# One opening transfer, half-width first products, a root on GpSimd and a new order in a fused attention and MLP kernel

## The chip, the cores and the metric

The kernel runs on one core of a Trainium2 chip. The metric is the device time of one execution in microseconds (us). The kernel before takes 588.61 us, the median of 3 runs (588.04 to 588.75). A core has five engines with an instruction queue each: TensorE (PE; its weight loads are listed as PEld), VectorE (DVE), ScalarE (ACT), GpSimd (POOL) and SyncE (SP), which issues the DMAs. An engine works through its queue in order, so an instruction that waits holds up all that stand behind it.

## The reference

Two batches of 768 tokens, 8 heads of 64. Attention is local (96 keys back) plus the first 8 keys, with a distance bias, then two feed-forward blocks of width 2048, the first with a scale and an offset:

```
n_global, n_local = (8, 96)
scores = scale * q @ k^T;  keep = is_global | is_local
bias = -slopes[:, None, None] * dist[None]
a = exp(where(keep, scores + bias, -1e9) - max) ;  a = a / (sum(a) + 1e-09)
x = (a @ v) laid out as [1536 tokens, 512]
r = max(x @ w_in, 0);   x = (s * (r * r) + b) @ w_out        # moe,  s and b are one number each
r = max(x @ w_in2, 0);  out = (r * r) @ w_out2               # moe2
```

## The kernel before, in words

**Tiles.** The 1536 tokens are 12 tiles of 128 rows; tiles 0 and 1 are the first of each batch and see 128 keys, the others 192. For each tile `qk` makes scores on PE, `ttr` adds the bias and takes the extreme on DVE, `exp` runs on ACT, `rsum` and `norm` divide, `tr` transposes on PE, `tput` copies the result out of PSUM (the tile `at`), `pv` multiplies by v, and `xhi`/`xlo` split the result in a high and a low part (`xh`, `xl`). Weights come as 64-bit numbers in 64 transfers of 512 KB (`st`), are decoded in four steps (`wdec`, steps 0 to 3), and split by `whi`/`wlo`. A product of split numbers is three matmuls: high by high, high by low, low by high.

**Stages.** The first four blocks of 128 columns of the first MLP (`h`, `relu`, `square`, `ghi`, `glo`, `y`, 256 tokens at a time) run woven into the attention, up to about 100 us; then the other blocks of both MLPs run by a seven-product scheme (`product`, 384 tokens) and its output matmuls (`y2`). The last output rows are finished one by one (`yrow`, six rows m of 128 tokens), added to what was kept (`flush2`) and stored.

**Order.** `order` lists every piece of work with its engines, an assumed cost, what it depends on and a due time; `Plan.run` places the pieces on the engines and so writes each engine's queue. `SHIFT` moves due times of single pieces, `PIN` binds a piece to an engine. Where PE has nothing to do before the first `h`, the planner writes small idle matmuls (`warm(0)`, 256 columns of zeros) into its queue. None of this is decided on the chip: there the queues run as they are written.

**The opening.** SP issues the transfer of n (L1408), then that of s and b (L1419), both spread over 128 partitions, then q and k of tile 0 (L410), the first weight block (L39), v and tile 1. DVE converts n (L1414 to L1416), starts the square root of s (`root`, L818 to L829), builds the bias planes (`consts`, L353 to L371), and then begins with `ttr` (L444).

Of the kernel before, what the change touches and what calls it, by code (L numbers as in the profile page):

```python
# [17 lines left out]
DM = H * D  # L18
DFF = 2048
P = 128  # L20
# [8 lines left out]
WARM, FILL = 8, 0.2  # L29
TB, SB = 768, 384  # L30
# [30 lines left out]
def decoded(a):  # L61
# [9 lines left out]
SHIFT = {('at', 2, 2): 28.4, ('at', 2, 3): 26.5, ('at', 3, 0): 33, ('at', 3, 1): 42, ('at', 4, 1): -16.3, ('at', 5,  # L71
    0): 6.4, ('at', 8, 0): 57.6, ('cadd', 14, 1, 1, 0): 225.2, ('cadd', 18, 0, 1, 0): 201, ('cadd', 20, 0, 1, 0):
    135.6, ('cadd', 26, 0, 0, 1): 288.3, ('cadd', 6, 0, 0, 1): 148.7, ('cadd', 8, 0, 0, 1): 237.2, ('check', 0):
# [21 lines left out]
    -34.3, ('ndh', 0, 3): -76.6, ('ndh', 0, 7): -33.3, ('ndh', 1, 0): 29.9, ('ndh', 1, 3): -2.7, ('ndh', 1, 5):  # L95
    -101.2, ('norm', 11, 3): -1.5, ('norm', 2, 1): -255.6, ('norm', 3, 1): -138.7, ('norm', 3, 2): 0.3, ('norm', 4,
# [1386 lines left out]
```

## Time and profile before

| what | us |
|---|---|
| median of 3 runs | 588.61 (588.04 to 588.75) |
| the profiled execution | 588.15 |
| its span, first to last event | 586.3 |
| PE busy (98% of the span) | 575.1 |
| DVE busy (84%) | 492.6 |
| ACT busy (61%) | 359.8 |
| POOL busy (16%) | 94.9 |

Busy shares are means over very different stretches, so they are read stage by stage: what stands still at the opening, which engines are full while attention and MLP are woven together, and what is left behind the last matmul. Matmuls overlap in their pipeline, so the time that one takes of PE is the distance between the starts of neighbours and not its own duration. The page's chain of waits is empty for this run; the bound is read from the stretches and from the timelines of the queues. The span does not hold 1.85 us of the execution's time.

### The profile page before, as it was taken

How to read it: one execution, taken by the hardware profiler on the slowest of the kernel's cores; microseconds unless marked ns; L12 is line 12 of the kernel's file. 1: busy time of each engine (PE TensorE's matmuls, PEld its weight loads, DVE VectorE, ACT ScalarE, POOL GpSimd, SP SyncE). 2: the span in 40 equal slices, each digit the busy share in tenths (PEclk: the TensorE clock that was granted, in tenths of full speed). 3: DMA queues.
4: the chain of work that ended last, by engine and by line, in shares of the span. 5: the costliest groups of instructions: out<-in, count | busy, mean ns of one | idle time of the engine just before them, and what ended most of it. 6: DMA issues, size and time to landing. Idle time of an engine off the chain costs nothing.

```text
span 586.3 us, 11064 instructions
## 1 busy us (share of the span) xinstructions
PE 575.1 (98%) x4125; PEld 520.3 (89%) x4125; DVE 492.6 (84%) x1139; ACT 359.8 (61%) x820; POOL 94.9 (16%) x176
## 2 busy tenths in 40 slices
PE   6999999999999999999999999999999999999997
PEld 4688988999989999999999989989899889989895
DVE  6999997699999899999989999899886987874443
ACT  4999987685766666556566666657454535444330
POOL 3653434101100000110000012120112011200000
PEclk9999999999999999999999999999999999999999
DMA  6876621032120332314021301323222131100023
GB/s 262 314 240 243 221 93 37 3 109 69 40 74 0 109 108 72 108 34 147 11 99 36 108 0 37 108 79 101 72 73 66 44 108 59 49 0 2 15 94 110
DMA packets 14888, 52.12 MB, mean 89 GB/s; under 512 B 1904, under 2 KB 2160, under 8 KB 14832
## 3 DMA queue, kind: packets, MB, share of 16 engines
q1 hardware_dynamic: 14832, 51.39, 25.8%
q8 instruction: 33, 0.54, 0.4%
q14 instruction: 23, 0.19, 0.1%
HBM read 48.24 MB, written 3.15 MB: 88 GB/s over the span
## 4 chain that ended last, share of the span: by engine, by line


## 5 line engine op out<-in xcount | busy, mean ns | idle before, releaser
L645 PE MATMUL h<-xh,u 128*128 128x384 f32 x448 | 130.5, 337 | 0.0
L748 PE MATMUL yy<-u,gh 128*128 128x512 f32 x360 | 111.9, 392 | 0.0
L645 PE MATMUL h<-th,u 128*128 128x384 f32 x336 | 99.6, 337 | 0.1
L742 PE MATMUL yy<-gh,u 128*128 128x512 f32 (+1 forms) x384 | 98.4, 337 | 0.0
L645 PEld LDWEIGHTS h<-xh,u 128*128 128x128 f32 x448 | 82.3, 188 | 1.1
L748 PEld LDWEIGHTS yy<-u,gh 128*128 128x128 f32 x360 | 67.0, 188 | 11.8
L645 PE MATMUL h<-xl,u 128*128 128x384 f32 x224 | 75.4, 336 | 0.0
L742 PEld LDWEIGHTS yy<-gh,u 128*128 128x128 f32 x384 | 66.7, 189 | 7.7
L748 PE MATMUL yy<-u,gl 128*128 128x512 f32 x180 | 70.3, 391 | 0.0
L742 PE MATMUL yy<-gl,u 128*128 128x512 f32 (+1 forms) x192 | 64.8, 338 | 0.3 <-DVE gl L719 0.3
L645 PEld LDWEIGHTS h<-th,u 128*128 128x128 f32 x336 | 62.0, 188 | 2.4 <-DVE u L666 0.8
L274 ACT ACTIVATE u<-st 128x512 fp32r<-128x512 f32 (+1 forms) x58 | 36.5, 634 | 39.1 <-DVE st L57 25.5
L645 PE MATMUL h<-tl,u 128*128 128x384 f32 x168 | 56.5, 336 | 0.0
L278 POOL TENSOR_SCALAR u<-st 128x512 fp32r<-128x512 f32 (+1 forms) x34 | 25.1, 739 | 171.9 <-PE h L645 61.8
L54 DVE SCALAR_TENSOR_TENSOR st<-st 128x512 int32<-128x512 int32 x64 | 45.1, 705 | 3.7 <-ACT gh L714 0.5
L274 ACT ACTIVATE st<-st 128x512 f32<-128x512 f32 x64 | 42.3, 677 | 7.7 <-DMA st<-in_moe_w_in_dram 3.8
L57 DVE SCALAR_TENSOR_TENSOR st<-st 128x512 int32<-128x512 int32 x64 | 44.1, 690 | 1.0
L645 PEld LDWEIGHTS h<-xl,u 128*128 128x128 f32 x224 | 42.1, 188 | 0.8
L452 ACT ACTIVATE sn<-sn,nm 128x192 f32<-128x192 f32 (+1 forms) x96 | 41.8, 444 | 0.2 <-DVE nm L444 0.2
L748 PEld LDWEIGHTS yy<-u,gl 128*128 128x128 f32 x180 | 33.8, 188 | 7.4
L666 DVE TENSOR_TENSOR u<-h,m 128x384 f32<-128x384 f32 x56 | 30.9, 552 | 11.2 <-PE h L645 10.0
L679 DVE TENSOR_TENSOR u<-h,u 128x384 f32<-128x384 f32 x56 | 30.9, 552 | 11.1 <-PE h L645 10.6
(163 smaller groups left out, 1206.9 us busy)
## 6 DMA issues: line engine op xcount, KB each, us to landing
st<-in_moe_w_in_dram SPq DMA_DIRECT2D x32, 512.0 KB, 4.3
st<-in_moe_w_out_dram SPq DMA_DIRECT2D x32, 512.0 KB, 3.6
q<-in_qk_dram SPq DMA_DIRECT2D x10, 768.0 KB, 5.3
v<-in_v_dram SPq DMA_DIRECT2D x10, 512.0 KB, 4.8
out_dram<-acc SPq DMA_DIRECT2D x11, 256.0 KB, 2.6
q<-in_qk_dram SPq DMA_DIRECT2D x2, 512.0 KB, 6.6
v<-in_v_dram SPq DMA_DIRECT2D x2, 256.0 KB, 7.2
out_dram<-acc SPq DMA_DIRECT2D x2, 128.0 KB, 2.0
```

What stands on the lines that cost most here:

```text
L54: nc.vector.scalar_tensor_tensor(out=lo, in0=hi, scalar=3, in1=lo, op0=ALU.logical_shift_left, op1=ALU.bitwise_or)
L57: nc.vector.scalar_tensor_tensor(out=lo, in0=hi, scalar=-(1 << 31), in1=lo, op0=ALU.bitwise_and, op1=ALU.bitwise_or)
L274: nc.scalar.activation(out=out, in_=in_, func=AF.Copy, scale=scale)
L278: nc.gpsimd.tensor_scalar(out=out, in0=in_, scalar1=scale, scalar2=0.0, op0=ALU.mult, op1=ALU.add)
L452: self.nc.scalar.activation(out=sn[:, x], in_=sn[:, x], func=AF.Exp, scale=-1.0, bias=self.nm[:, n, h:h + 1], accum_out=self.rs[:, n, h:h ...
L645: self.nc.tensor.matmul(ps, p, q, start=first and kt == 0 and x == 0, stop=kt == 1 and x == 2, skip_group_check=not first)
L666: self.nc.vector.tensor_tensor(out=t, in0=self.T["h", a, tp, 1], in1=self.T["m1", a, tp], op=ALU.add)
L679: self.nc.vector.tensor_tensor(out=self.T["r", a, tp, c, side], in0=self.T["h", a, tp, bank], in1=m, op=ALU.add)
L742: self.nc.tensor.matmul(yj, p[:, js], q[:, lo:hi], start=first and x == 0 and not (side and j % 2), stop=last and x == 2 and not (side and ...
L748: self.nc.tensor.matmul(y[m], p[:, ms], q, start=first and x == 0, stop=last and x == 2)
```

## The change

- **One opening transfer.** n, s and b are written by the host in front of the first half of tile 0's q and k, in each of 128 rows of 528 words (`head`). It is the first transfer; the second half of tile 0 and the two halves of tile 1 follow as transfers of 512 columns. The two small transfers of n and of s and b are gone. The planes take n from a conversion of two words (`low`); the exact conversion of n moves to the check near the end; GpSimd copies the six words aside (`keep`), since the buffer is used again.
- **Scores of tiles 0 and 1 in two halves** of four heads each; each half needs its own half of the transfer.
- **Bias planes**: one DVE instruction less in the first group, and the root of s is off DVE but for two instructions; it is 18 instructions on GpSimd, by another iteration that needs no reciprocal.
- **First products in two parts.** For the first two blocks w = 0 and 1, `h` of tokens 0 to 255 is made as two times 12 matmuls of 128 columns, the first part (tile 0 alone) as a piece of its own (`h0`).
- **`rsum` in two pieces**: the addition may go to GpSimd (14 of 24 do), the reciprocal stays on DVE. **Decode step 0** may go to GpSimd (19 of 64 do).
- **Last output row** m = 5: its last two blocks are summed in two fresh PSUM banks, 256 columns each; what was summed before is added to the kept rows ahead of that (`pre`), and each half is added and stored by itself.
- **The order is planned anew**, with another `SHIFT`, `PIN`, `CFG` and other assumed costs.

```diff
-SHIFT = {('at', 2, 2): 28.4, ('at', 2, 3): 26.5, ('at', 3, 0): 33, ('at', 3, 1): 42, ('at', 4, 1): -16.3, ('at', 5,
+SHIFT = {('at', 4, 2): -23.3, ('cadd', 16, 1, 0, 1): -19.1, ('cadd', 18, 0, 0, 1): -4.4, ('cadd', 22, 0, 1, 1):
...
-            nc.vector.tensor_scalar(out=k, in0=k, scalar1=self.nl, scalar2=None, op0=ALU.subtract)
-            nc.vector.tensor_tensor(out=key[:, 0, :], in0=dist[:, 0, :], in1=k, op=ALU.max)
+            nc.vector.scalar_tensor_tensor(out=key[:, 0, :], in0=k, scalar=nl, in1=dist[:, 0, :], op0=ALU.subtract,
+                                           op1=ALU.max)
...
+                if n == 0:
+                    self.T["few"] = t[:, 0:6].bitcast(I32)
+                    self.T["qk", n] = t[:, FEW:FEW + 2 * DM]
+                    start(out=t[:, 0:FEW + DM].bitcast(I32), in_=self.head)
+                    return
...
-            s = [self.psa().rearrange("p (x t) -> p x t", x=4) for _ in range(2)]
-            for hp in range(4):
+            s = [self.psa()[:, 0:2 * P].rearrange("p (x t) -> p x t", x=2) for _ in range(2)]
+            c = self.T["qk", n].rearrange("p (f a x t) -> p f a x t", a=2, x=2, t=P)[:, hf]
+            for x in range(2):
...
-    def rsum(self, n, hf):
+    def rsum(self, n, hf, step, e):
         rs = self.rs[:, n, 4 * hf:4 * hf + 4]
-        self.nc.vector.tensor_scalar(out=rs, in0=rs, scalar1=1.0e-9, scalar2=None, op0=ALU.add)
-        self.nc.vector.reciprocal(out=rs, in_=rs)
+        if step:
+            self.nc.vector.reciprocal(out=rs, in_=rs)
+        elif e == "vector":
+            self.nc.vector.tensor_scalar(out=rs, in0=rs, scalar1=1.0e-9, scalar2=None, op0=ALU.add)
+        else:
+            self.nc.gpsimd.tensor_scalar(out=rs, in0=rs, scalar1=1.0, scalar2=1.0e-9, op0=ALU.mult, op1=ALU.add)
...
+    def h(self, w, lo, hi, part=None):
+        if part != 1:
+            self.T["h", w, lo] = self.psH.tile([P, 512], F32, tag="h", name=f"h{w}_{lo}")
+        ps = self.T["h", w, lo]
+        c0, c1 = (0, hi - lo) if part is None else (part * P, part * P + P)
...
-            nc.vector.reciprocal(out=t[:, 1:2], in_=rt)
-            nc.vector.scalar_tensor_tensor(out=rt, in0=t[:, 0:1], scalar=t[:, 1:2], in1=rt, op0=ALU.mult, op1=ALU.add)
-            nc.vector.tensor_scalar(out=rt, in0=rt, scalar1=0.5, scalar2=None, op0=ALU.mult)
+        elif step < 5:
+            u = t[:, 1:2]
+            nc.gpsimd.tensor_tensor(out=u, in0=t[:, 0:1], in1=rt, op=ALU.mult)
+            nc.gpsimd.tensor_tensor(out=u, in0=u, in1=rt, op=ALU.mult)
+            nc.gpsimd.tensor_scalar(out=u, in0=u, scalar1=-0.5, scalar2=1.5, op0=ALU.mult, op1=ALU.add)
+            nc.gpsimd.tensor_tensor(out=rt, in0=rt, in1=u, op=ALU.mult)
...
-        add(("d0", w, i), "ACT:0.58", lambda e, a=(w, i): f.wdec(*a, 0, e), [("lw", w, i)], key)
+        add(("d0", w, i), "ACT:0.58 POOL:0.66", lambda e, a=(w, i): f.wdec(*a, 0, e), [("lw", w, i)], key)
...
+    for x in range(2):
+        add(("h0", x), {"PE": 0.77}, lambda e, x=x: f.h(x, 0, 256, 0), xdone(0) + [("wlo", x, 0)] + [("h0", 0)] * x,
+            use[x] + cfg["moe"] - 9, acq=[("h", x, 0)])
...
+            pre = ("fl", g[0], tp, 5, 2)
+            add(pre, "DVE:0.6", lambda e, g=g, tp=tp: f.flush2(g, tp, 5, 0, e), [yprev], tc + span - 8)
+            for m, lo, hi in [(m, 0, DM) for m in range(5)] + [(5, 0, 256), (5, 256, DM)]:
```

The three places below are those that the prediction speaks of. The first is the opening of DVE's queue. Before, these rows stand there (`sb` holds s and b, `acc` the planes that are being built, `nv` the converted n):

```order
L1416 SCALAR_TENSOR_TENSOR nv<-nf 128x2
L384 MEMSET idle 128x256
L818 TENSOR_SCALAR sg<-sb 128x1
L819 TENSOR_SCALAR sg<-sg 128x1
L820 TENSOR_TENSOR tmp<-sb,sg 128x1
L821 TENSOR_TENSOR sgb<-sb,sg 128x1
L822 TENSOR_SCALAR rt<-tmp 128x1
L824 TENSOR_SCALAR rt<-rt 128x1
L827 RECIPROCAL tmp<-rt 128x1
L828 SCALAR_TENSOR_TENSOR rt<-tmp,rt 128x1
L829 TENSOR_SCALAR rt<-rt 128x1
L353 TENSOR_SCALAR acc<-acc,nv 128x128
```

Now DVE's queue opens with these (`low` is n, from the first words of tile 0's buffer):

```order
L1463 MEMSET warm 128x1
L391 MEMSET idle 128x256
L1473 CAST low<-q_143 128x2
L360 TENSOR_SCALAR acc<-acc,low 128x128
L362 TENSOR_SCALAR acc<-acc,low 128x128
L363 TENSOR_TENSOR acc<-acc 128x128
L364 SCALAR_TENSOR_TENSOR acc<-acc,low 128x128
L282 TENSOR_SCALAR ND_138<-acc 128x128
```

The nine instructions of the root that stood between n and the planes are gone, and the memset that PE waits for comes first, ahead of all that waits for a transfer.

The second place is ACT's queue between the exponentials of tiles 0 and 1 and the first `h`. Before (`at_0` to `at_3` are copies out of PSUM, `sn` scores, `st` weight blocks in decode step 0, `xh` the result's high part; a row whose `sn` reads `rs` is `norm`):

```order
L452 ACTIVATE sn_1_372,rs<-sn_1_372,nm 128x192 x2
L482 COPY at_0_412<-a 128x512
L518 CAST xh<-a 128x4x128
L274 ACTIVATE st_0_197<-st_0_197 128x512
L274 ACTIVATE st_1_202<-st_1_202 128x512
L482 COPY at_1_452<-a 128x512
L452 ACTIVATE sn_2_445,rs<-sn_2_445,nm 128x192 x2
L452 ACTIVATE sn_3_455,rs<-sn_3_455,nm 128x192 x2
L518 CAST xh<-a 128x4x128
L482 COPY at_0_501<-a 128x384
L274 ACTIVATE sn_3_455<-sn_3_455,rs 128x192 x2
```

Now:

```order
L280 ACTIVATE sn_0_217<-sn_0_217,rs 128x128 x4
L280 ACTIVATE ND<-acc 128x192
L500 COPY at_0_369<-a 128x512
L280 ACTIVATE u_78<-st_0_168 128x512
L280 ACTIVATE st_0_187<-st_0_187 128x512
L500 COPY at_0_399<-a 128x512
L466 ACTIVATE sn_0_377,rs<-sn_0_377,nm 128x192 x2
L466 ACTIVATE sn_1_391,rs<-sn_1_391,nm 128x192 x2
L466 ACTIVATE sn_2_435,rs<-sn_2_435,nm 128x192 x2
L536 CAST xh<-a 128x4x128 x2
L466 ACTIVATE sn_3_441,rs<-sn_3_441,nm 128x192 x2
L280 ACTIVATE sn_1_391<-sn_1_391,rs 128x192 x2
```

From the first exponential to the `norm` that PE's last transposes ahead of `h` wait for, ACT loses three pieces (a copy of 512 columns, a decode step, a copy of 384) and gains two (four `norm` of 128 columns and one plane of 192, `ND`); the rest only changes its order.

The third place is PE's queue around the first `h`. Before, four groups of three transposes of tile 2 stand ahead of it, the last two right before it:

```order
L474 MATMUL a<-ident,sn_2_445 128x2x64
L475 MATMUL a<-ident,sn_2_445 128x128
L476 MATMUL a<-ident,sn_2_445 128x128
L474 MATMUL a<-ident,sn_3_455 128x2x64
L475 MATMUL a<-ident,sn_3_455 128x128
L476 MATMUL a<-ident,sn_3_455 128x128
L799 MATMUL h_0_529<-xh,u_82 128x256
```

Now two of the four groups stand ahead of it, and its matmuls have half the columns:

```order
L492 MATMUL a<-ident,sn_0_377 128x2x64
L493 MATMUL a<-ident,sn_0_377 128x128
L494 MATMUL a<-ident,sn_0_377 128x128
L450 MATMUL a<-q_215 64x192 x8
L492 MATMUL a<-ident,sn_1_391 128x2x64
L493 MATMUL a<-ident,sn_1_391 128x128
L494 MATMUL a<-ident,sn_1_391 128x128
L825 MATMUL h_0_511<-xh,u_78 128x128
```

The other two groups moved behind the first part of `h`. The idle matmuls ahead of the first `h` go from 52 to 46.

## Rows read from the trace of the kernel before

**Rows 1.** The page's first part: busy us, share of the span, instructions.

```profile
PE 575.1 (98%) x4125; PEld 520.3 (89%) x4125; DVE 492.6 (84%) x1139; ACT 359.8 (61%) x820; POOL 94.9 (16%) x176
```

**Rows 2.** Stretches in us: busy us per engine, granted clock, DMA share, GB/s.

```profile
20.00:30.00 10.00, 9.49 (x118) 7.01 (x114) 9.02 (x38) 10.00 (x34) 4.68 (x11) 1.00 0.67 233
30.00:40.00 10.00, 10.00 (x202) 8.71 (x199) 9.86 (x38) 9.60 (x34) 5.64 (x10) 1.00 0.75 246
```

**Rows 3.** Timeline, SP's first DMAs: start us, us, engine, line, operation.

```profile
0.81 0.38 SPq L1408 DMA_DIRECT2D ni<-in_n_dram  x1
1.36 0.34 SPq L1419 DMA_DIRECT2D sb<-in_sb_dram  x1
```

**Rows 4.** DMA rate from 2 to 10 us, in 40 slices of 0.2 us.

```profile
GB/s 2 2 2 2 2 0 0 0 0 0 0 21 83 21 62 42 41 62 389 369 348 492 471 328 410 471 430 348 492 379 348 399 420 492 399 389 471 451 348 389
```

**Rows 5.** Timeline of DVE at the opening, idle time and its releaser in brackets.

```profile
3.38 0.17 DVE L1414 CAST nf<-ni 128x4 f32<-128x4 int32 x1 [2.45 <-DMA ni<-in_n_dram]
...
6.13 0.15 DVE L818 TENSOR_SCALAR sg<-sb 128x1 f32<-128x1 f32 x1 [1.91 <-DMA sb<-in_sb_dram]
...
7.60 0.28 DVE L353 TENSOR_SCALAR acc<-acc,nv 128x128 f32<-128x128 f32 x1
...
8.20 0.28 DVE L357 TENSOR_SCALAR acc<-acc,nv 128x128 f32<-128x128 f32 x1
```

**Rows 6.** Timeline of ACT from the planes to the first h.

```profile
10.42 0.80 ACT L274 ACTIVATE ND<-acc 128x192 bf16<-128x192 f32 x2 [0.88 <-DVE acc L370]
11.13 0.68 ACT L274 ACTIVATE st<-st 128x512 f32<-128x512 f32 x1
11.70 0.38 ACT L452 ACTIVATE sn<-sn,nm 128x128 f32<-128x128 f32 x1
...
21.19 0.58 ACT L482 COPY at<-a 128x512 f32<-128x512 f32 x1
21.65 0.59 ACT L518 CAST xh<-a 128x512 fp32r<-128x512 f32 x1
...
25.98 0.49 ACT L482 COPY at<-a 128x384 f32<-128x384 f32 x1
26.35 0.82 ACT L274 ACTIVATE sn<-sn,rs 128x192 f32<-128x192 f32 x2
27.05 0.69 ACT L274 ACTIVATE st<-st 128x512 f32<-128x512 f32 x1
```

**Rows 7.** Timeline of PE: the last transposes and the first h.

```profile
27.40 0.27 PE L474 MATMUL a<-ident,sn 128*128 128x128 f32 x1
27.51 0.27 PE L475 MATMUL a<-ident,sn 128*128 128x128 f32 x1
...
27.64 0.37 PE L799 MATMUL h<-xh,u 128*128 128x256 f32 x1
...
27.96 0.40 PE L799 MATMUL h<-xh,u 128*128 128x256 f32 x2
28.20 0.28 PE L799 MATMUL h<-xl,u 128*128 128x256 f32 x1
```

**Rows 8.** Weight loads by shape: count, busy us, mean ns, idle before.

```profile
L799 PEld LDWEIGHTS h<-xh,u 128*128 128x128 f32 x192 | 31.0, 188 | 0.9 <-issue 0.3 <-ACT acc L274 0.3
...
L475 PEld LDWEIGHTS a<-ident,sn 128*128 128x128 f32 x40 | 5.6, 141 | 0.3 <-POOL sn L278 0.3
...
L494 PEld LDWEIGHTS a<-at,v 128*64 128x64 f32 x32 | 1.7, 136 | 0.5 <-ACT at L482 0.3
```

**Rows 9.** Timeline of the tail: the last rows' additions on DVE.

```profile
580.59 0.69 DVE L789 TENSOR_TENSOR acc<-yy,acc 128x512 f32<-128x512 f32 x1 [0.68 <-PE yy L757]
...
581.97 0.76 DVE L789 TENSOR_TENSOR acc<-yy,acc 128x256 f32<-128x256 f32 x2 [0.69 <-PE yy L757]
```

**Rows 10.** GpSimd's instructions by shape, mean ns.

```profile
L278 POOL TENSOR_SCALAR u<-st 128x512 fp32r<-128x512 f32 x30 | 22.8, 763 | 121.3 <-PE h L645 61.8 <-DVE st L57 27.4 <-DVE st L558 16.8
...
L278 POOL TENSOR_SCALAR ND<-acc 128x128 bf16<-128x128 f32 x3 | 0.9, 310 | 6.2 <-DVE acc L358 6.0
```

More of the change, by code (lines that the diff above doesn't have):

```diff
@@ L29 @@
 WARM, FILL = 8, 0.2
+FEW = 16
 TB, SB = 768, 384
@@ L252, in run @@
                     if dma:
-                        queue = max(free[e] + 0.9, queue) + dma
-                        seen = queue + 1.2
+                        queue = max(free[e] + 0.6, queue) + dma
+                        seen = queue + 1.0
                     heapq.heappush(events, free[e])
@@ L267, in run @@
                 now = max(now, heapq.heappop(events))
-        self.time = max(max(free.values()), queue + 1.2)
+        self.time = max(max(free.values()), queue + 1.0)
 def copy_r(nc, eng, out, in_, scale=1.0):
@@ L362, in consts @@
                                     op0=ALU.logical_shift_left)
[L363 removed]
+            nc.vector.tensor_scalar(out=far[:, 1, 0:n], in0=nr[:, 1, 0:n], scalar1=nl, scalar2=-NEG, op0=ALU.is_ge,
                                     op1=ALU.mult)
@@ L398, in heads, with load @@
         return range(4 * g, 4 * g + 4) if n < 2 else range(2 * g, 2 * g + 2)
-    def load(self, what, n):
+    def load(self, what, n, half=0):
         b, i = n % 2, n // 2
@@ L404, in load @@
         if what == "q":
-            t = self.qp.tile([P, 3, 4, P], F32, tag="q", name=f"q{n}")
-            self.T["q", n] = t[:, 0]
-            self.T["k", n] = t[:, 1:3] if n < 2 else t[:, 1:3].rearrange("p a h t -> p (a h t)").rearrange(
-                "p (h t) -> p h t", h=KT)
-            a = slice(0, a.stop + 1)
-            start(out=t[:, a], in_=self.qk_[b, i, :, a])
+            if half == 0:
+                t = self.qp.tile([P, 3 * DM], F32, tag="q", name=f"q{n}")
+                self.T["q", n], self.T["k", n] = t[:, 0:DM].rearrange("p (h t) -> p h t", h=KT), t[:, DM:3 * DM].rearrange(
+                    "p (h t) -> p h t", h=KT)
+                if n == 0:
[3 more added lines that the diff above has]
+                    return
+                self.T["qk", n] = t
+            c = slice(half * DM, half * DM + DM) if n < 2 else slice(0, 3 * DM)
+            start(out=self.T["qk", n][:, c], in_=self.qk_[b, i, :, c])
         else:
@@ L729, in ybanks, with y2 @@
         return self.T["y", tp]
-    def y2(self, a, tp, c, side, first, last, new):
+    def y2(self, a, tp, c, side, first, last, new, five):
         y = self.ybanks(tp, new)
@@ L747, in y2, with yrow @@
                 for x, (p, q) in enumerate(((gh, oh), (gh, ol), (gl, oh))):
-                    self.nc.tensor.matmul(y[m], p[:, ms], q, start=first and x == 0, stop=last and x == 2)
-    def yrow(self, a, tp, m):
-        y = self.T["y", tp]
+                    self.nc.tensor.matmul(y[m], p[:, ms], q, start=first and x == 0,
+                                          stop=(last or five and m == 5) and x == 2)
+    def yrow(self, a, tp, m, cols=None):
+        if cols is None:
+            y, n, first = self.T["y", tp][m], slice(0, DM), False
+        else:
+            n, first = cols, True
+            y = self.T["yh", cols.start] = self.psH.tile([P, 512], F32, tag="h", name=f"yh{cols.start}")[:, cols]
         ms = slice(m % 3 * P, (m % 3 + 1) * P)
@@ L756, in yrow @@
             for x, (p, q) in enumerate(((gh, oh), (gh, ol), (gl, oh))):
-                self.nc.tensor.matmul(y[m], p, q, start=False, stop=c == 1 and x == 2)
+                self.nc.tensor.matmul(y, p, q[:, n], start=first and c == 0 and x == 0, stop=c == 1 and x == 2)
     def flush2(self, grp, tp, j, part, e, cols=slice(0, DM)):
@@ L788, in flush2 @@
         else:
-            nc.vector.tensor_tensor(out=a, in0=self.T["y", tp][j][:, cols], in1=a, op=ALU.add)
-    def h(self, w, lo, hi):
-        ps = self.psH.tile([P, 512], F32, tag="h", name=f"h{w}_{lo}")
-        self.T["h", w, lo] = ps
+            y = self.T["yh", cols.start] if part == 3 else self.T["y", tp][j][:, cols]
+            nc.vector.tensor_tensor(out=a, in0=y, in1=a, op=ALU.add)
+    def h(self, w, lo, hi, part=None):
[3 more added lines that the diff above has]
+        c0, c1 = (0, hi - lo) if part is None else (part * P, part * P + P)
         xh, xl = self.X
@@ L798, in h @@
             for x, (a, b) in enumerate(((ih, xh), (ih, xl), (il, xh))):
-                self.nc.tensor.matmul(ps[:, 0:hi - lo], a[:, kt * P:(kt + 1) * P], b[:, kt, lo:hi],
-                                      start=(kt == 0 and x == 0), stop=(kt == KT - 1 and x == 2))
+                self.nc.tensor.matmul(ps[:, c0:c1], a[:, kt * P:(kt + 1) * P], b[:, kt, lo + c0:lo + c1],
+                                      start=(kt == 0 and x == 0 and part != 1), stop=(kt == KT - 1 and x == 2),
+                                      skip_group_check=part == 1)
     def gtile(self, what, w, lo, hi):
@@ L962, in order @@
                 w = (n, g)
-                last = hf == 1 if not two else x == 1
+                last = not two or x == 1
                 add(("ttr",) + w, "DVE:0.57" if two else "DVE:0.85", lambda e, w=w: f.ttr(*w),
                     [("qk",) + su] + [("ndh", int(two), h) for h in (range(2 * g, 2 * g + 2) if two else range(4 * g, 4 * g + 4))] +
-                    [("ttr", n, g - 1)] * last, t,
+                    [("ttr", n, g - 1)] * (two and last), t,
                     acq=[("sN",) + w], rel=[("a", "s", x) + su for x in range(2)] * last)
@@ L983, in order @@
     xdone = lambda n: [("xl", n, y) for y in range(1 if n < 2 else 2)]
-    for x in range(5):
-        add("sq" if x == 4 else ("root", x), "DVX:0.9" if x == 0 else "DVX:0.5", lambda e, x=x: f.root(x),
-            [("root", x - 1)] if x else ["sb"], cfg["root"])
-    add("sb", "SP:0.47", lambda e: f.load_sb(), key=-895.0, dma=0.06)
+    for x in range(6):
+        add("sq" if x == 5 else ("root", x), "DVX:0.36" if x == 1 else "POOL:0.6", lambda e, x=x: f.root(x),
+            [("root", x - 1)] if x else ["nd2", "keep"], cfg["root"])
     add("second", "SP:0", lambda e: f.second(), [d for n in range(NTILE) for d in xdone(n)], 0.0)
@@ L1087, in order @@
         tm, fin = t + cfg["moe"], lo == NT - 256
-        add(("h",) + u, {"PE": 1.43}, lambda e, u=u: f.h(*u, u[1] + 256), dh, tm, acq=[("h",) + u],
+        part = 1 if lo == 0 and w < 2 else None
+        add(("h",) + u, {"PE": 0.77 if part else 1.43}, lambda e, u=u, part=part: f.h(*u, u[1] + 256, part),
+            dh + [("h0", 1)] * (part is not None), tm, acq=[] if part else [("h",) + u],
             rel=[slot(w, 0, x) for x in "hl"] * fin)
@@ L1131, in order @@
         if u == (26, 0):
-            add(("check", 0), "DVE:0.35", lambda e: f.check(0), ["second"], tc - 20)
+            add(("check", 0), "DVE:0.9", lambda e: f.check(0), ["second"], tc - 20)
             add(("check", 1), {"PE": 0.15}, lambda e: f.check(1), [("check", 0), prev], tm, acq=[("h", "chk")])
@@ L1394, in body @@
 @with_exitstack
-def body(ctx, tc, n, s_b, qk, v, wi1, wo1, wi2, wo2, out):
+def body(ctx, tc, head, qk, v, wi1, wo1, wi2, wo2, out):
     nc = tc.nc
```

213 lines of the change are left out of this document (118 added, 95 removed), and 120 rows, old and new, of tables (PIN, SHIFT).

## The prediction

> **What bounds the kernel now.** I read the busy shares first [rows 1]: PE is busy 98% of the span. That is a mean, so the stretches come next [rows 2]. The reader is to see two regimes there. From 30 to 40 us PE is busy 10.00 of 10 us, and it stays so to the tail; its clock is granted at 1.00, the higher of its two levels. From 20 to 30 it is busy 9.49, but part of that is idle matmuls that the planner wrote in to pass the time, and the full engine is ACT (10.00), with DVE at 9.02. So the execution is an opening, whose length ACT and DVE set, then 554 us of PE work without holes, then a tail. From the first `h` at 27.64 [rows 7] on, nothing can be won but what takes work from PE; what brings the first `h` forward shortens the execution one for one, if PE stays full behind it.
>
> The opening is read from three queues. SP issues n at 0.81 and s and b at 1.36 [rows 3]. The rate of the DMAs shows what follows [rows 4]: 2 GB/s for a microsecond, nothing for another, 21 to 83 up to 5.6 us, and only then about 400. The two transfers, 2 KB and 1 KB spread over 128 partitions, keep the data of tile 0 behind them until 5.6. On DVE n arrives at 3.38, but the queue then stands 1.91 us for s and b, until 6.13, since the root comes before the planes; the planes begin at 7.60 [rows 5]. On ACT the first exponential runs at 11.70, and from there to the last `norm` before the first `h`, which ends where the next instruction starts, at 27.05, there is no gap to speak of [rows 6]: ACT is the chain of the opening.
>
> **The change part by part.**
>
> *The opening transfer and the root.* The new first transfer has 128 rows of 2112 bytes, 270 KB. At some 400 GB/s [rows 4] that is 0.7 us. The first bytes of n moved at about 2 us, so the head lands at 3.5 by my estimate: 2.2, since a hint stands ahead of the issue, 0.7 of data, and 0.6 for a cold start. No row shows a large transfer as the first one. The bounds: 3.0 if there is no cold start; 6.1, where s and b land now, if the slow start belongs to the DMA engines and not to the small rows. I take 3.5, near n's 3.38, the only transfer that starts cold.
>
> DVE then converts (0.17) and begins the planes at 3.7, not at 7.60. Between the planes and the first exponential 4.10 us lie now (7.60 to 11.70) [rows 5, 6]. One DVE instruction of 0.28 goes [rows 5], and one of ACT's two 192-column planes, 0.36 (10.42 to 11.13 for two) [rows 6]. So the first exponential starts at 3.7 + 4.10 - 0.64 = 7.2, 4.5 us earlier. The weight block that ACT decodes just ahead of it is the fourth transfer: 270 and 262 and 262 KB stand before its 512, 1.3 MB in all, landing at 2.2 + 3.3 + 0.6 = 6.1, ahead of ACT's turn for it.
>
> *ACT up to the first `h`.* From first exponential to the end of that `norm` it is 15.35 us now (11.70 to 27.05). Three pieces go: a copy of 512 columns (0.46, 21.19 to the next start at 21.65), a decode step (0.57, 11.13 to 11.70) and a copy of 384 (0.37, 25.98 to 26.35) [rows 6]. Two come: the one plane, 0.36, and four `norm` of 128 columns; two of 192 take 0.70 (26.35 to 27.05), a plane of 192 0.36, so four lie between 1.0 and 1.4, and I take 1.2. Sum +0.15 (bounds -0.05 to +0.35). From the end of that `norm` to the first `h` 0.59 pass (27.05 to 27.64) [rows 6, 7]. New first `h`: 7.2 + 15.35 + 0.15 + 0.59 = 23.3, that is 4.34 earlier. The halved scores of tiles 0 and 1 have the same matmuls as before, and the DVE pieces that feed ACT are early enough: the first half's `ttr` begins when the planes are done, about 0.6 before ACT is free.
>
> *PE work that lies behind that point.* Two of the four groups of tile 2's transposes moved behind it: 2 x 3 x 0.11 (27.40 to 27.51) [rows 7] = +0.66.
>
> *The first products in two parts.* Before, w = 0 and 1 take 12 matmuls of 256 columns each, 0.12 us apart (two from 27.96 to 28.20) [rows 7], 2.88 in all. Now it is 48 matmuls of 128 columns, each with its own 128-column weight load. No row has this shape. From below: half of 0.12, 0.06, 2.9 in all, +0.0. From above: 0.12 as now, 5.8, +2.9. The weight load decides. The loads of this kind take 188 ns, those of 64 columns 136 [rows 8]; 52 ns for 64 columns more makes about 104 ns for the 128, and with columns that stream in 0.06 the load is the longer of the two. The transposes, with 128 weight columns and 128 moving ones, come every 0.11 us [rows 7]; theirs is the nearest row, and I take it: 48 x 0.11 = 5.3, +2.4. Against it speaks that the load of a transpose takes only 141 ns with the same shape [rows 8], so loads of 128 columns are not all slow.
>
> The Trainium skill says the same of the load in TensorE: Matmul & The Clock Gate, section LDWEIGHTS (loading the stationary operand): its time is the number of weight columns over 1.2, in ns, whatever the rows. By that page a part of 12 would take 12 x 107 = 1.3 us (an estimate from the page), against 0.7 if columns alone counted. The difference of 52 ns per 64 columns in the rows above agrees with it.
>
> *GpSimd.* The root is 18 small instructions there; its cheapest arithmetic in the trace, 128 columns, takes 0.31 us [rows 10], a bound from above for one column; below is 0.1. Four come early and hide behind the exponentials; thirteen come after a `norm`, 1.3 to 4 us, and the first `relu` that needs the root comes only after the first `h`. At nothing; if the cover is gone, the additions of `rsum` queued behind come late, which is the second rival below. The decode steps given to GpSimd take 0.76 [rows 10] and free ACT of 19 pieces of 0.57, on stretches where PE is the bound: nothing.
>
> *The tail.* A row of six matmuls takes 1.38 (580.59 to 581.97) [rows 9]; the last now has twelve of 256 columns at 0.12: +0.06. Behind PE two additions took 0.76; one of 0.38 is left: -0.38. The addition put ahead of it lies in DVE's idle time of 0.68 a row. The copy of the six words, the exact conversion at the check, the other queue order behind 100 us: nothing, PE is full and DVE has room; a wait that they open would show as a hole in PE.
>
> **Sum.** -4.34 + 0.66 + 2.4 - 0.32 = -1.6. The profiled execution took 588.15 (span 586.3 and 1.85 around it), 0.46 under the median of the runs, 588.61; 588.15 - 1.6 gives **586.5**.
>
> **The rivals.**
>
> *The short matmuls go at their columns' pace.* For it: the transposes' load of 141 ns, and that spacing has followed columns in all rows so far. Against it: 188 against 136. The parts then cost 0.0 to +0.2 (0.064 apart), and the time is 588.15 - 4.34 + 0.66 + 0.2 - 0.32 = 584.4.
>
> *GpSimd holds DVE up (slower).* Fourteen additions of `rsum` now stand in GpSimd's queue behind `norm`, decode steps and `gh`, and DVE's reciprocal waits for each, with all of DVE's queue behind it. Place: 15 to 80 us. Price: if each waits for one GpSimd instruction, 0.5 to 0.76 us [rows 10], twelve of them behind the first `h` make 6 to 9 us on DVE, which from 30 to 40 has 0.14 of 10 us free [rows 2]; PE then stands for the part beyond what ACT's relief and the earlier start give, 4 to 5 us: 591. It decides from a mean wait of 0.3 us on. Against it: an addition needs only the exponentials before it, and there GpSimd is busy 4.68 and 5.64 of 10 us, so it is often free.
>
> *The head does not land early.* The slow rise of the rate is a cold start and not the small rows; then the head lands at 6.1, the first `h` comes 2.6 later than I say: 589.1. Against it: the 2 GB/s phase has exactly the two small transfers in it, and the rate is full from one slice to the next [rows 4].
>
> **How the numbers follow.** Forecast 0.47 (586.5, its own range 585.5 to 587.6), short matmuls fast 0.28 (584.4), GpSimd 0.12 (591), late head 0.08 (589.1), rest 0.05. A measurement of this kernel can tell 0.2%, 1.2 us, from no change: faster means under 587.4. The forecast gives that with 0.8, the first rival always: 0.66. Slower, over 589.8, comes from most of the GpSimd case and a third of the late head: 0.14. The rest is 0.20. The range leaves out the lower third of the first rival and the GpSimd case: 584.0 to 589.4.
>
> **What would show it.** In the profile after: DVE's planes begin near 3.7, the first exponential near 7.2, the first `h` near 23.3; starts of the 128-column `h` matmuls 0.11 apart (0.06 by the first rival); PE 10.00 of 10 us from 30 on; one addition of 0.38 behind the last matmul. A first `h` later than 25, or holes in PE between 30 and 100, with DVE's reciprocals waiting for GpSimd, would make the prediction wrong.

## The result, and the profile after

The changed kernel takes 592.65 us, the median of 6 runs (591.09 to 596.36), against 588.47 (588.00 to 588.97) for the kernel before beside it: a ratio of 1.0078, 95% interval 1.0058 to 1.0098. It is slower by 4.2 us; I had forecast 586.5. The profiled execution took 591.24, with a span of 589.5, 3.2 longer than before [rows 1].

```profile
PE 578.4 (98%) x4149; PEld 523.7 (89%) x4149; DVE 500.7 (85%) x1122; ACT 347.2 (59%) x792; POOL 125.5 (21%) x224
```

PE is busy 98% as before, and 3.3 us more. GpSimd took 31 us more, ACT 13 less. The stretches answer to [rows 2] (columns as there):

```profile
20.00:30.00 10.00, 8.48 (x148) 6.72 (x144) 8.03 (x32) 9.57 (x34) 5.56 (x14) 1.00 0.69 243
30.00:40.00 10.00, 10.00 (x152) 8.87 (x153) 8.03 (x30) 8.30 (x32) 5.32 (x10) 1.00 0.76 264
40.00:50.00 10.00, 9.45 (x106) 7.83 (x107) 9.06 (x32) 9.33 (x31) 5.17 (x11) 1.00 0.50 176
60.00:70.00 10.00, 9.86 (x149) 8.66 (x147) 7.04 (x31) 6.66 (x21) 3.05 (x5) 1.00 0.86 312
70.00:80.00 10.00, 9.39 (x140) 8.12 (x144) 9.26 (x31) 9.97 (x37) 7.60 (x14) 1.00 0.42 128
```

The prediction's own signs of error are there: the first `h` is later than 25 (below), and PE has holes behind it, 1.3 us in all from 30 to 100. From 60 to 70 DVE and ACT stand too (7.04 and 6.66 of 10): there no engine is full, and they wait for each other and for transfers.

**The opening**, by the timelines of DVE, ACT and PE, answers to [rows 5 to 7]:

```profile
3.76 0.17 DVE L1473 CAST low<-q 128x2 f32<-128x2 int32 x1 [2.54 <-DMA q<-in_head_dram]
4.04 0.29 DVE L360 TENSOR_SCALAR acc<-acc,low 128x128 f32<-128x128 f32 x1
...
8.02 0.68 ACT L280 ACTIVATE st<-st 128x512 f32<-128x512 f32 x1 [0.62 <-DMA st<-in_moe_w_in_dram]
8.60 0.39 ACT L466 ACTIVATE sn<-sn,nm 128x128 f32<-128x128 f32 x1
...
23.32 0.33 PE L492 MATMUL a<-ident,sn 128*128 128x128 f32 x1 [1.44 <-POOL sn L284]
...
25.21 0.31 PE L825 MATMUL h<-xh,u 128*128 128x128 f32 x1
25.35 0.28 PE L825 MATMUL h<-xl,u 128*128 128x128 f32 x1
25.46 0.39 PE L825 MATMUL h<-xh,u 128*128 128x128 f32 x2
```

The head is used at 3.76 and the planes begin at 4.04, nearly as forecast (3.5 and 3.7). The first exponential comes at 8.60, not at 7.2: ACT waits for the first weight block, which lands at 8.0. I had counted on some 400 GB/s; from 2 to 10 us the DMAs moved 323 on average, and 113 to 174 from 4.6 to 5.8. The first `h` is at 25.21, 2.4 earlier than before and 1.9 later than forecast. Ahead of it PE stands 1.44 for a `norm` on GpSimd; GpSimd's timeline, with one row of DVE, shows why:

```profile
17.18 0.18 POOL L856 TENSOR_TENSOR tmp<-tmp,rt 128x1 f32<-128x1 f32 x1
...
21.23 0.67 POOL L284 TENSOR_SCALAR st<-st 128x512 f32<-128x512 f32 x1
21.98 0.20 POOL L476 TENSOR_SCALAR rs<-rs 128x4 f32<-128x4 f32 x1
22.49 1.18 POOL L284 TENSOR_SCALAR sn<-sn,rs 128x192 f32<-128x192 f32 x2 [0.31 <-DVE rs L472]
...
22.22 0.18 DVE L472 RECIPROCAL rs<-rs 128x4 f32<-128x4 f32 x1 [1.52 <-POOL rs L476]
```

The last exponential of that half ends at 20.7. The addition starts at 21.98, behind the root (17.18 to 21.2) and a decode step; DVE waits 1.52 for it.

**Behind the first `h`** the chain of waits, which was empty before, says what ended last (start, us, what):

```profile
25.45 1.29 PE h L825 x12
...
30.02 0.33 SPq L426
30.45 6.41 DMA st<-in_moe_w_in_dram
...
37.62 0.69 POOL u L284
38.34 1.14 DVE u L559
39.50 3.89 DMA st<-in_moe_w_in_dram
43.54 0.68 POOL st L284
44.22 2.32 POOL sn L284 x4
46.58 0.33 PE a L493
...
59.06 0.33 SPq L426
59.49 7.23 DMA st<-in_moe_w_out_dram
66.80 0.91 POOL st L284
67.73 0.69 DVE st L55
...
69.63 1.27 POOL sn L284 x2
70.94 0.33 PE a L493
```

Twice it is the same figure, with the blocks that land at 43.4 and 66.7: a weight block is issued late, lands 3.9 or 7.2 us after, GpSimd's decode step waits for it, and the `norm` that PE needs comes behind that step: in GpSimd's own queue at 43.4, by way of DVE's next decode step at 66.7. The block that lands at 36.9 acts on the next transfer: a split (`u`) stands in GpSimd's queue where it waits for that block, and only when the split and its DVE half are done, at 39.5, is the block of 43.4 issued.

Added up from PE's starts (span +3.2): first `h` -2.4; `h` products +2.8 (48 of 128 columns take 5.64); transposes +2.9, of which 0.66 was forecast; the rest -0.1; the tail 0.0, from the start of the last matmul to the end 4.75 against 4.79. At the waits of 46 and 70 PE is idle for 0.48, 0.25 and 0.50, and around these waits its starts stand 2.1 further apart than elsewhere, 0.4 of it booked under `h`. One addition of 0.42 stands behind PE, as forecast:

```profile
585.07 0.42 DVE L813 TENSOR_TENSOR acc<-yh,acc 128x256 f32<-128x256 f32 x1 [0.28 <-PE yh L780]
```

but the last stores of 128 KB took 2.6 us to land against 2.0 (median of two), which ate it. A term of 0.3 can hardly be read here: in the profiles of the changed kernel and of its edits below, none of which touches the tail, the same stretch takes 4.6 to 6.0.

### The profile page after: what moved, and what is told of

The parts are those of the page before. It is cut to its first block, busy times and chain, and to the rows that moved or that the text cites. A ratio compares the mean times of both kernels' runs of the same rounds, so it can differ in the third digit from the quotient of the medians.

```text
span 589.5 us, 11132 instructions
## 1 busy us (share of the span) xinstructions
PE 578.4 (98%) x4149; PEld 523.7 (89%) x4149; DVE 500.7 (85%) x1122; ACT 347.2 (59%) x792; POOL 125.5 (21%) x224
## 4 chain that ended last, share of the span: by engine, by line
PE 80%; DVE 10%; DMA 4%; POOL 2%; issue 1%; ACT 1%; SPq 0%; POOLq 0%; DVEq 0%
PE h L663 32%; PE yy L766 21%; PE yy L760 14%; DVE tq L635 3%; DMA st<-in_moe_w_in_dram 3%; PE y L910 3%; PE h L825 3%; PE a L450 2%; PE a L528 1%; DMA st<-in_moe_w_out_dram 1%; PE yy L780 1%; POOL sn L284 1%; PE a L524 1%; ACT sn L466 1%; DVE st L55 1%
## 5 line engine op out<-in xcount | busy, mean ns | idle before, releaser
L280 ACT ACTIVATE u<-st 128x512 fp32r<-128x512 f32 (+1 forms) x59 | 37.7, 645 | 49.2 <-DVE st L58 24.9
L280 ACT ACTIVATE st<-st 128x512 f32<-128x512 f32 x45 | 30.4, 678 | 25.4 <-DMA st<-in_moe_w_in_dram 10.9
L825 PE MATMUL h<-xh,u 128*128 128x256 f32 (+1 forms) x208 | 41.4, 288 | 0.0
```

Of the source, the lines that this page charges most:

```text
L280: nc.scalar.activation(out=out, in_=in_, func=AF.Copy, scale=scale)
L825: self.nc.tensor.matmul(ps[:, c0:c1], a[:, kt * P:(kt + 1) * P], b[:, kt, lo + c0:lo + c1], start=(kt == 0 and x == 0 and part != 1), stop ...
```

## The experiments

The planner's order is taken as a list of pieces, and only this list (or a line or two of code) is edited, so that nothing is planned anew; `move(seq, names, after)` takes the named pieces out of the list and puts them behind `after`. Theory 1: GpSimd's queue holds DVE and PE. Theory 2: weight blocks that land late set the time.

**The base.** No edit.

> The changed kernel once more, with nothing edited, as the base for the other runs of this set. Its profiled execution of before took 591.24 us at a granted clock of 1.00; its other executions went up to 596.36, and the lower the granted clock of the whole execution (0.992 to 0.999), the longer they took. If the spread is TensorE's clock, executions at 0.992 lie near 591.2 / 0.992 = 596 and those at 1.00 near 591 here too, and a profile that catches one shows a stretch at the lower level, at some place where PE stood still just before. If the spread is something else (DMA, the order in which transfers land), time and clock do not go together.

592.61 (592.06 to 593.01), ratio 1.0066 (1.0053 to 1.0079), all at 0.998 to 1.000 of the clock. The slowdown is there with hardly any loss of clock; the spread of the first six runs (granted clocks of 0.992 to 1.000) came from the clock in part, of which more below. The base's profile (592.06) has its first `h` at 25.87, 0.7 later than that of the changed kernel above with the same code, since its first weight block lands 0.6 later (first exponential at 9.22); so the first `h` of an edit is best counted from the first exponential, 16.6 in both.

**The root later.**

```diff
+    return move(seq, [("root", 2), ("root", 3), ("root", 4), "sq"], ("norm", 2, 3))
```

> The root's four iteration pieces on GpSimd (13 instructions, 17.18 to 21.23 us in the changed kernel) are put behind the last norm of tile 2 in GpSimd's queue, where it stands idle from 25.8 to 28.1; all else keeps its order. Theory 1 (GpSimd's queue holds DVE and PE): the sum of tile 2 is ready at 20.7 but its addition runs only at 21.98, behind the root and a decode step; now the addition runs at about 20.9, DVE's wait of 1.52 before the reciprocal goes, the norm on GpSimd ends 1.0 earlier, the hole of PE of 1.44 ahead of tile 2's transposes shrinks to under 0.5 and the first h comes at 24.5 in place of 25.2: 0.7 to 1.0 less in the time. Theory 2 (ACT is the chain of the opening, and GpSimd only happens to wait beside it): the first h stays within 0.2 of 25.2, and the time does not move.

The first `h` comes at 24.43, 15.7 behind the first exponential and so 0.9 earlier, as theory 1 has it; but the time is 596.24 (592.49 to 598.59), ratio 1.0128 (1.0101 to 1.0154), its fastest run no better than the base. The next piece behind the root is now late, the split of a weight block:

```profile
30.27 0.33 PE L825 MATMUL h<-xh,u 128*128 128x128 f32 x1 [1.11 <-POOL u L284]
```

What was won at 25 is lost at 30. The runs above 595 had a granted clock of 0.987 to 0.991.

**The additions on DVE.**

```diff
+    return [(n, "DVE" if n[0] == "re" else e, fn) for n, e, fn in seq]
```

> The 14 additions of rsum that the change gave to GpSimd go back to DVE, at the place in the order where they stood; all else as in the changed kernel. Theory 1 in the form of the prediction's second rival (the additions wait in GpSimd's queue and hold DVE's reciprocals): of DVE's waits for an addition, 2.2 us in three places (0.41, 0.29, 1.52), all go, PE's hole at 21.9 to 23.3 shrinks by 1, and the time falls by 0.7 to 1.5; DVE pays 14 x 0.2 = 2.8 us, of which only what lies on the path counts. Theory 2 (the additions are not the cause; the other pieces on GpSimd, norm and decode steps, are): the holes of PE at 46 and 70 us stay as they are (0.48, 0.25 and 0.50), and the time falls by the opening's part alone, 0.7 at most.

592.07 (591.20 to 592.99), ratio 1.0053 (1.0040 to 1.0066). The first `h` comes at 24.45, 16.1 behind the first exponential (8.30), but PE's hole at 46 grows from 0.48 to 1.28 and the two at 70 from 0.75 to 1.21; theory 2 had them stay. The additions hold the first `h` by 0.5; they are not what sets the time.

**Decode steps 0 on ACT.**

```diff
+    return [(n, "ACT" if n[0] == "d0" else e, fn) for n, e, fn in seq]
```

> The 19 decode steps 0 that the change gave to GpSimd go back to ACT, at the place in the order where they stood. Theory 1 (decode steps on GpSimd stand ahead of a norm that PE waits for): at 43.5 one of 0.68 stands right ahead of the norm that PE waits for at 46.2, and at 66.8 one waits 4.4 for its weight block with an addition and a norm behind it; the holes of 0.48, 0.25 and 0.50 go, and the time falls by 1.0 to 1.3. Theory 2 (the weight blocks land late, whoever decodes them): ACT then waits in GpSimd's place, with exponentials queued behind, the hole at 70 stays or grows, and the time moves by under 0.5 or rises; seven steps before 75 us cost ACT 7 x 0.57 = 4 us, in a stretch where it is 7 to 10 of 10 us busy.

592.78 (591.62 to 594.61), ratio 1.0074 (1.0058 to 1.0090). The hole at 46 goes, and ACT waits in GpSimd's place for the block that lands at 66.8, with a copy behind it that PE needs (PE's waits: in all, times, longest):

```profile
PE a L528 <- ACT at L500: 1.9, 2, 1.6
```

Theory 2 said this: whoever decodes, the queue behind the step waits for the block.

**Whole first products.**

```diff
-        add(("h0", x), {"PE": 0.77}, lambda e, x=x: f.h(x, 0, 256, 0), xdone(0) + [("wlo", x, 0)] + [("h0", 0)] * x,
+        add(("h0", x), {"PE": 0.77}, lambda e, x=x: f.h(x, 0, 256), xdone(0) + [("wlo", x, 0)] + [("h0", 0)] * x,
...
-        add(("h",) + u, {"PE": 0.77 if part else 1.43}, lambda e, u=u, part=part: f.h(*u, u[1] + 256, part),
+        add(("h",) + u, {"PE": 0.77 if part else 1.43}, lambda e, u=u, part=part: None if part else f.h(*u, u[1] + 256),
```

> The first products of w = 0 and 1 are made whole: 12 matmuls of 256 columns at the place where the first part of 12 matmuls of 128 stood, and nothing where the second part stood. In the changed kernel the low part of tile 1's result is ready at 24.2 us, while the first part starts at 25.2, so the whole product should find its input there. Theory 1 (the parts are PE work for nothing: 48 matmuls at 0.113 against 24 at 0.119): 2.6 to 2.8 us of PE work go, the first h stays within 0.3 of 25.2, and the time falls by 2.0 to 2.8. Theory 2 (up to 71 us the time is set by weight blocks that land late, at 36.9, 43.4 and 66.7, and not by PE's work): PE only waits longer, the holes at 46 and 71 grow by what is saved, and the time falls by under 0.8.

593.25 (592.25 to 594.58), ratio 1.0079 (1.0063 to 1.0094): 2.5 us of PE work less bring nothing, PE waits instead (3.0 in three places for `norm` on GpSimd, 0.9 and 0.5 for `gh` and `gl`). Theory 2, up to 71 us.

**Three blocks ahead of q and v.**

```diff
+    return move(seq, [("lq", 9), ("lv", 8)], ("lw", 5, 0))
```

> In SP's queue the transfers of q for tile 9 and of v for tile 8 (issued at 57.4 and 59.1 in the changed kernel) go behind the three weight blocks issued at 59.5 to 60.4; nothing else moves. Theory 2 (weight blocks that land late set the time up to 71): the first block lands at about 64 in place of 66.7, GpSimd's decode step, the addition and the norm behind it come 2.7 earlier, the holes at 70 to 71.5 (0.25 and 0.50) go, and the time falls by 0.5 to 0.8; not more, since the hole at 46 lies before. Theory 1 (GpSimd's queue itself is too slow): the block comes earlier, but the hole stays over 0.5, time within 0.3.

590.98 (590.33 to 595.07), ratio 1.0057 (1.0034 to 1.0081). The three blocks land at 58.5, 61.5 and 64.1 in place of 66.7, 68.0 and 69.2, earlier than expected, and the holes at 71 are gone; the one at 46 is 1.04. By the medians the time is 1.6 under the base, by the means and by PE's starts in the two profiles 0.6, and the intervals overlap. By the medians it is the largest step of any single edit, and it is on SP's queue.

**Small transfers, each row with its own address, and all rows from one.**

```diff
+        nc.sync.dma_start(out=few0[:, 0:4], in_=head[:, 0:4])        # first run; 4:6 likewise
+        nc.sync.dma_start(out=few0[:, 0:4], in_=head[0:1, 0:4].to_broadcast([P, 4]))    # second
```

> Two transfers of 128 rows of 16 and of 8 bytes, as before the change, are put ahead of the opening transfer, into words that nothing reads. Theory of the prediction (the small rows hold the DMA queue until about 5.6): the head lands at 6.0 to 6.3 in place of 3.76, DVE's planes begin at 6.3 to 6.6, the first exponential comes at 10.3 to 11 in place of 8.6, the first h 1.5 to 2.4 later. Rival (the slow rise is the DMA engines' cold start, whatever comes first): the head lands about 0.9 later, by the two issues of 0.4 to 0.5, and the first h under 1 later.

> As the run with two small transfers ahead of the opening transfer, but all 128 rows of 16 and of 8 bytes are read from one and the same row of DRAM, as the kernel before reads n, s and b; in the earlier run each row had its own address, and the opening transfer landed at 4.66 in place of 3.80, no more than its later issue. Theory A (128 reads of one address hold the DMAs up): the opening transfer lands at 5.5 to 6.5, the first exponential comes at 10.3 to 11.3, the first h 1.5 to 2.5 later than in the changed kernel. Theory B (the small transfers have nothing to do with the late data of the kernel before; it is the place of the branch hint, which stood between the two, or some other thing): it lands at 4.5 to 4.9 again, and the time is that of the run with own addresses, 593 to 594.

When the head is there, with own addresses and then from one address, on DVE:

```profile
4.66 0.17 DVE L1473 CAST low<-q 128x2 f32<-128x2 int32 x1 [3.44 <-DMA q<-in_head_dram]
```

```profile
6.63 0.17 DVE L1473 CAST low<-q 128x2 f32<-128x2 int32 x1 [5.42 <-DMA q<-in_head_dram]
```

and the DMA rate of the second from 0 to 10 us, in slices of 0.25:

```profile
GB/s 0 0 0 0 0 0 0 1 2 2 2 2 1 0 0 0 51 93 77 60 51 68 270 411 396 410 402 402 442 442 442 410 426 385 369 410 402 418 401 402
```

It is the picture of [rows 4]. Small rows alone cost the 0.9 of their two issues; 128 reads of one address hold the DMAs up by 2.0 more. My mechanism (small rows) was wrong in this point, theory A right. The first `h` comes at 26.15 and 27.34. The times are 593.90 (ratio 1.0081, 1.0066 to 1.0097) and 595.16 (1.0118, 1.0103 to 1.0134).

The profile with own addresses (596.30) caught PE's clock at its lower level. PE stands 1.43 us for the same `norm`, up to 24.26; then, by stretches of 1 us (PE busy first, granted clock third from the end):

```profile
23.00:24.00 1.00, 0.00 (x0) 0.00 (x0) 0.84 (x3) 1.00 (x4) 0.69 (x2) 1.00 1.00 399
...
26.00:27.00 1.00, 1.00 (x7) 1.00 (x7) 1.00 (x8) 0.88 (x4) 0.77 (x2) 0.59 0.98 401
...
32.00:33.00 1.00, 1.00 (x26) 1.00 (x24) 1.00 (x9) 0.92 (x4) 0.00 (x0) 0.50 0.49 49
33.00:34.00 1.00, 1.00 (x45) 0.86 (x42) 1.00 (x5) 0.25 (x2) 0.00 (x0) 0.99 0.70 221
```

0.50 is 1.2 GHz; from 26.2 to 33.0 PE ran at it: the instructions from 26.38 to 33.06, 6.7 us, take 3.6 in the changed kernel's profile at the higher level (25.35 to 28.97), and the 128-column matmuls of `h` among them stand 0.21 apart. The run of whole products has such a stretch from 47.4 to 50.8, behind a stand of 1.34 and a shorter one. The same stand of 1.44 in the changed kernel's profile was followed by 1.00 throughout: the loss comes in some executions only, and where it comes the holes cost more than in that profile. All executions with a granted clock under 0.996 are of the changed kernel or of an edit that leaves PE a stand of over a microsecond (down to 0.987); the kernel before, the four moves and the six edits below have none under 0.997.

**Five edits together, and four.**

```diff
+    seq = move(seq, [("root", 1)], ("d1", 0, 0))
+    seq = move(seq, [("root", 2), ("root", 3)], ("root", 1))
+    seq = move(seq, [("root", 4)], ("re", 1, 0))
+    seq = move(seq, ["sq"], ("re", 1, 1))
+    seq = move(seq, [("d0", 3, 0)], ("norm", 4, 3))
+    seq = move(seq, [("lq", 9), ("lv", 8)], ("lw", 5, 0))
+    return move(seq, [("d0", 0, 0)], ("exp", 0, 0))
```

The first run has the whole first products too (the edit shown above); the second leaves them in parts.

> Five edits together, each on a wait of the changed kernel: whole first products as in the run with them alone; the root's iteration spread over GpSimd's idle time ahead of 15 us (its DVE step right behind the first decode step); the decode step of block (3, 0) on GpSimd behind the two norms of tile 4 that PE waits for at 46; the three blocks ahead of q of tile 9 and v of tile 8; and the first decode step on ACT behind the first four exponentials. If the losses named so far are the ones and add up (2.7 of PE work, 0.7 to 1.2 in the first h, 0.5 at 46, 0.75 at 71), the time falls by 4 to 5, to 587 or 588 by the base run of 592.6, and is below the kernel before. If a wait behind them takes their place, as when the root was moved alone, it stays above 590.

> The four moves of the run with five edits (root spread over GpSimd's idle time, the decode step of block (3, 0) behind the norms, three blocks ahead of q and v, first decode step behind four exponentials), but the first products left in their two parts. With whole products and the four moves the time was 588.4; whole products alone brought nothing (593.3 against 592.6). If whole products are worth their 2.7 us of PE work once PE no longer waits, this run comes at 590.5 to 591.1. If the moves did all of it, it comes at 588.0 to 589.0.

588.41 (587.15 to 590.12), ratio 0.9997 (0.9987 to 1.0007), and with the parts 587.99 (587.83 to 588.57), ratio 0.9991 (0.9982 to 1.0000). The four moves alone give the whole slowdown back: 4.6 us by the medians, 4.4 by the ratios, each against the kernel before run beside it. Of the four only the one on SP's queue was also run alone (1.6 at most); the root was moved alone in another form, the two decode steps not at all. By PE's starts in the profiles of the base and of the four moves, 2.2 of the 4.5 us lie ahead of the first `h` and 2.3 behind it, where no hole of PE is left up to 100 us. Of the 2.2, 1.9 come from the first exponential, which no longer stands behind ACT's decode of the first block (four moves; 9.22 in the base):

```profile
7.32 0.39 ACT L466 ACTIVATE sn<-sn,nm 128x128 f32<-128x128 f32 x1
```

The first `h` is at 23.69 and 23.63, 0.4 from my 23.3. Whole products did not add to it in the first run, because a new wait opened there, of PE for `gh` in GpSimd's queue:

```profile
38.69 0.38 PE L910 MATMUL y<-gh,u 128*128 128x256 f32 x1 [1.23 <-POOL gh L891]
39.57 0.38 PE L910 MATMUL y<-gl,u 128*128 128x256 f32 x1 [0.49 <-DVE gl L896]
```

**A sixth edit.**

```diff
+    seq = move(seq, [("d0", 2, 0), ("d0", 2, 1)], ("gh", 1, 0))
```

> The five edits, and a sixth: the decode steps of blocks (2, 0) and (2, 1) on GpSimd go behind the high part of the products of w = 1 (gh). In the run with five edits PE stands 1.23 at 37.8 to 39.0 for that high part, which waits in GpSimd's queue behind decode steps whose block lands at 35.7, and then 0.49 for the low part on DVE. Theory (work that PE needs stands behind a decode step that waits for its weight block): the 1.23 go, the 0.49 may grow to at most 1.0, since a split on GpSimd and one on DVE are still ahead of it; the time falls by 0.7 to 1.7, to 586.7 to 587.7, below the kernel before. Rival (another wait takes its place again): 588.2 or more.

586.49 (586.24 to 587.03), ratio 0.9965 (0.9953 to 0.9977): faster than both kernels, and 1.9 under the five edits, a little more than expected. PE has 69.8 of the 70 us from 30 to 100 (70.0 before, 68.7 in the changed kernel):

```profile
30.00:100.00 70.00, 69.80 (x1062) 60.97 (x1061) 64.16 (x238) 63.34 (x216) 31.31 (x60) 1.00 0.48 166
```

Now that PE hardly waits, the 128-column parts cost what their spacing says: against the run with four moves, the products of `h` take 36.38 in place of 38.84, 2.46 less, and the time is 1.5 lower with a first `h` 0.2 later. The two runs differ in the sixth edit as well, which was not run with the parts; but the wait for `gh` that it removes is not there in the run with four moves.

**The kernel before with rows of their own.**

```diff
-                      in_=n.bitcast(I32).rearrange("(o a) -> o a", o=1).to_broadcast([P, 4]))
+                      in_=n.bitcast(I32))
...
-        load_sb = lambda: nc.sync.dma_start(out=sb, in_=s_b.rearrange("(o a) -> o a", o=1).to_broadcast([P, 2]))
+        load_sb = lambda: nc.sync.dma_start(out=sb, in_=s_b)
```

> The kernel before, with one edit: n and the pair s, b lie in DRAM as 128 equal rows, so that each partition reads an address of its own; every queue stays word for word as before. By the two runs with small transfers, reads of one address held the DMAs until 5.6 and cost the opening 2.0 us. Theory 1 (in the kernel before PE is full from the first h on, so an earlier first h counts one for one): s and b land at 3.6 to 4.2 in place of 6.1, the planes on DVE begin at 5.1 to 5.8 in place of 7.6, the first h comes 1.8 to 2.4 earlier than 27.64, and the time falls by 1.6 to 2.3. Theory 2 (weight blocks and queues further on set the time in the weave there too, as in the changed kernel): first h earlier by as much, but holes of PE open between 30 and 100 and the time falls by under 0.8.

587.15 (586.11 to 587.85), ratio 0.9979 (0.9970 to 0.9988). The planes begin at 4.68, 2.9 earlier than in [rows 5]; the exponentials then wait, by way of `ttr`, for the scores of tile 0, which stand on PE behind 17 idle matmuls that end at 8.9:

```profile
4.68 0.28 DVE L353 TENSOR_SCALAR acc<-acc,nv 128x128 f32<-128x128 f32 x1
```

```profile
10.59 0.40 ACT L452 ACTIVATE sn<-sn,nm 128x128 f32<-128x128 f32 x1 [1.73 <-DVE nm L444]
```

```profile
26.87 0.36 PE L799 MATMUL h<-xh,u 128*128 128x256 f32 x1
```

The first `h` is 0.8 earlier, not 1.8 to 2.4, but it counts one for one: PE's last matmul starts 0.75 earlier, PE stays at 10.00 of 10 from 30 to 100, no hole opens. Theory 1 of that run, with the size halved.

## Why the prediction was wrong

- **The step that failed** is the premise that PE stays full behind the first `h`. By it the prediction put the root on GpSimd "At nothing" and the decode steps given to GpSimd, "on stretches where PE is the bound", at "nothing", and it has no term for the new order ahead of 100 us. I took a property of the old order, that PE has no holes from 30 on, for one of the stage. In the new order pieces that PE needs stand behind decode steps that wait for transfers, and PE waits. The four moves show it: they change only the order of a few pieces on four queues, take no work away, and bring 4.6 us.
- **The miss in terms.** Between the forecast of -1.6 and the +3.2 of the span lie 4.8 us: 1.9 in the opening, 2.3 in the transposes beyond the 0.66 (most of it at the waits of 46 and 70), 0.4 in the products of `h`, 0.3 in the tail. With the four moves, and so without the waits, the sum holds: by PE's starts against the kernel before, the first `h` is 4.0 earlier (4.34 forecast), the products of `h` take 2.4 more (2.4), the transposes 1.0 more (0.66).
- **The second rival** (591, GpSimd holds DVE) named the engine and nearly the time of the profile, 591.24, but that is luck: of its fourteen additions DVE waits for three (0.41, 0.29 and 1.52), all ahead of the first `h`, not for twelve behind it. With the additions on DVE the median falls by 0.5, within the intervals. The waits that count are `norm` and `gh` behind decode steps whose blocks come late; I had priced GpSimd's instructions, not the transfers that they wait for.
- **The opening.** Head and planes came nearly as forecast (3.76 for 3.5, 4.04 for 3.7). The weight block, which I had at 6.1, landed at 8.0, and ACT's decode of it stood ahead of the first exponential; with that decode behind four exponentials they start at 7.3 to 7.5 (7.2 forecast). From there to the first `h` 16.6 passed, not 16.1, for the wait of the addition: with the additions on DVE it is 16.1. So -2.4 came in place of -4.34. That wait stands behind the root, whose thirteen instructions behind the `norm` took 4.05 us (17.18 to 21.23), at the upper end of my 1.3 to 4; the addition stood behind them and a decode step.
- **The cause of the slow start** was the shared address, not the small rows; the rival "the head does not land early" was wrong for the changed kernel either way.
- **The first products** cost nearly what I said: +2.5 to 2.8 by their spacing, 2.4 forecast; the 48 stand 0.118 apart in the mean, twelve of them in the chain 0.11. The first rival (0.06) is out; what I put down for it, that spacing had followed the columns in all rows, did not hold in [rows 7], where transposes of 128 columns stand 0.11 apart and products of 256 stand 0.12. That the weight load sets this spacing was argued: no run varies the load by itself. The Trainium skill's rule in TensorE: Matmul & The Clock Gate, section LDWEIGHTS (loading the stationary operand), by which 12 such matmuls would take 1.3 us (an estimate from the page), agrees with the 1.29 of the chain at 25.45. At the lower clock such matmuls stood 0.21 apart, twice what that rule gives. Whether the cost is on the path depends on PE being full: at 592 its removal bought nothing, at 588, together with the sixth edit, 1.5.
- **The tail**: -0.32 forecast, 0.0 came. The addition went, the store took longer; a term of this size is within what the tail differs from profile to profile.
- **The median** lies 1.4 above the profiled execution. Two things that I had no term for are seen in other executions: the clock that falls behind a hole in some, and the first weight block, which in the base's profile lands later still (first exponential at 9.22). How much each adds to the median is not shown.

What stays open: how much each of the four moves gives, alone or with the other three in place; why the DMAs slow down from 4.6 to 5.8; and why the last store takes longer.

## What to carry to other kernels

A stage without holes is a property of its order: when the order is written anew, follow each piece that the full engine waits for back through its queue, and price not the instructions ahead of it but the transfer that the slowest of them waits for. Waits in series take turns: an edit that removes one of them can show nothing in the time (the root moved alone won 0.9 at 25 and lost it at 30; 2.5 us less PE work bought nothing), so try them together before a cause is dropped. Put steps that wait for a transfer behind those that do not.

## What the runs showed of the hardware

- 128 rows of 16 and of 8 bytes read from one DRAM address delayed the transfer queued behind them by 2.0 us more than the same rows with addresses of their own (head used at 6.63 against 4.66).
- Time to landing differed with what was still moving ahead: three blocks of 512 KB issued from 59.5 to 60.4 behind q and v landed one after the other, at 66.7, 68.0 and 69.2, the first 7.2 us after its issue; one issued at 39.5 behind a single transfer of q took 3.9.
- A stand of PE of 1.4 us was followed by 6.8 us at the lower clock in one execution and by none in another.
- Matmuls of 128 columns with a weight load of 128 columns each start about 0.11 us apart at the higher clock and 0.21 at the lower.
